# A linear-attention and mixture-of-experts kernel on one core: the order of its first part comes from a planner written into the kernel, and some of its transfers are merged or cut

## The chip, the core and the metric

The kernel runs on one core of one Trainium2 chip. The core has a matrix engine (TensorE, PE in the profile), a vector engine (VectorE, DVE), a scalar engine (ScalarE, ACT), a general engine (GpSimd, POOL) and an engine that here only issues transfers (SyncE, SP). Each engine runs its own list of instructions strictly in the order in which it was built; an instruction whose input is not there yet holds up everything behind it on that engine. The metric is device time in microseconds (us); lower is better. The number to predict is the median of several runs.

## What is computed

The reference is linear attention, a gated two-matrix product, and a layer of eight experts of which each token uses one:

```python
proj = einsum('bhsd,df->bhsf', x, w_phi)                 # for x = q and x = k
proj = proj - max(abs(proj), axis=-1)
phi  = concat([exp(proj), exp(-proj)])                   # q_p and k_p
kv, z = einsum('bhsf,bhsd->bhfd', k_p, v), sum(k_p, axis=2)
x = (q_p @ kv) / (q_p @ z + 1e-6)                        # 8 batches, 8 heads, 576 tokens of 64
x = ((x @ w1) * (x @ w2) @ w3) @ w_out                   # 4608 tokens of 512, inner width 1024
gate = softmax(x @ w_gate)                               # 8 experts, the largest one is used
out[tokens of e] = gate * (relu(x @ e_w1[e]) @ e_w2[e])  # inner width 1024
```

## The kernel before

To keep float32 accuracy with 16-bit matmuls, every operand is held as two float16 halves (high and low), and each product is three matmuls. ScalarE writes a high half, VectorE computes the low half as value minus high half; so most steps are a pair ScalarE, then VectorE.

The program has two parts. **The first part** runs four units of two batches. Each unit has four attention groups of two heads (`group`): q, k and v are loaded, split into halves on VectorE (`split`, lines 491 and 493, tile `sp`), turned by a transposing transfer (line 499, tiles `Tkf` and `Tqf`), projected on TensorE, exponentiated on ScalarE (`e`, `k`, `q`, lines 554 and 556; their low halves on VectorE, line 561), and multiplied (`kv`, `nm`, `nx`). The float32 tiles of k and of q share one buffer (`tag="kqf", bufs=1`), so the load of one waits for the splits of the other. Three blocks of the gated product (`moe1`) follow each unit, a unit later: `pab` on TensorE (lines 806 to 808), `asb`, `gf`, `gt` on ScalarE and VectorE, then `py` (line 843), its copy `yb` out of the accumulator by ScalarE (line 850), and rows of 2052 bytes that are stored to memory (`rows_d`, lines 940 and 943). Beside both, `expert_weight` prepares the sixteen expert matrices: a 2 MB load into the one buffer `wf` (line 296), squares for a scale (line 302), then eight pieces `pc`, high half on ScalarE (line 321), low half on VectorE (line 325), stored to a scratch tensor `wscr` (line 327). Four buffers of one piece each hold `pc`. **The second part** (`phase_b`, lines 1127 to 1183) runs forty slots of 128 tokens through the experts with weights loaded back from `wscr` (`wb`, 4 MB each); the first two of these loads are issued before the first part has ended. Its order is written out by hand.

In the first part each step is recorded with a time of its own, `at(t, fn)`, from the table `O`; the steps are traced in the order of these times. The framework then schedules: whenever an engine is free in its cost model, the ready instruction that was traced earliest is taken. What comes out is a fixed list for each engine. All transfers but the gathers and scatters go out from SyncE, in one list too.

## Time and profile before

| what | value |
|---|---|
| runs of the kernel | 1642.35, 1636.98, 1639.8 us; median 1639.8 |
| profiled execution, its own time | 1653.94 us |
| its span, first to last instruction | 1652.2 us |
| mean granted clock of TensorE | 0.936 of full speed |
| TensorE, VectorE, ScalarE busy over the span | 86%, 61%, 53% |
| transfers issued by SyncE in the change's reach | 16 loads `wf`, 128 stores `wscr`, 128 large loads of q and k |

The profile was taken in one execution, whose own time is 14 us above the median; differences worked out from it are taken off the median. The busy shares are means over two very different parts: in the first VectorE and TensorE are both loaded, in the second TensorE alone. They say little until they are read stretch by stretch.

### The profile page before, as it was taken

How to read it: one execution, taken by the hardware profiler on the slowest of the kernel's cores; microseconds unless marked ns; L12 is line 12 of the kernel's file. 1: busy time of each engine (PE TensorE's matmuls, PEld its weight loads, DVE VectorE, ACT ScalarE, POOL GpSimd, SP SyncE). 2: the span in 40 equal slices, each digit the busy share in tenths (PEclk: the TensorE clock that was granted, in tenths of full speed). 3: DMA queues.
4: the chain of work that ended last, by engine and by line, in shares of the span. 5: the costliest groups of instructions: out<-in, count | busy, mean ns of one | idle time of the engine just before them, and what ended most of it. 6: DMA issues, size and time to landing. Idle time of an engine off the chain costs nothing. (4 is left out here: it accounts for less than half of the span.)

```text
span 1652.2 us, 38216 instructions
## 1 busy us (share of the span) xinstructions
PE 1428.4 (86%) x14850; PEld 1032.2 (62%) x14854; DVE 1001.4 (61%) x3031; ACT 881.7 (53%) x1979; POOL 226.9 (14%) x491
## 2 busy tenths in 40 slices
PE   5988877888898796889697998968949999999998
PEld 4665555666665474657475766636746777777775
DVE  6998899987898696879697898434411111111111
ACT  4786688777786685768576777335201111111111
POOL 3313100010111010100101000100102111121110
PEclk9988777998999798999898999979979999999999
DMA  7845245575767775574955665963346346747351
GB/s 200 237 125 157 73 124 100 153 124 126 134 170 124 123 166 66 159 146 115 149 159 97 161 101 139 188 191 116 51 145 193 76 83 172 250 104 178 78 170 31
DMA packets 273043, 225.16 MB, mean 136 GB/s; under 512 B 187221, under 2 KB 244825, under 8 KB 271706
## 3 DMA queue, kind: packets, MB, share of 16 engines
q1 hardware_dynamic: 265306, 202.71, 53.5%
q0 software_dynamic: 7552, 19.97, 4.2%
q8 instruction: 118, 1.93, 0.6%
q14 instruction: 67, 0.55, 0.2%
HBM read 261.22 MB, written 53.67 MB: 191 GB/s over the span
## 5 line engine op out<-in xcount | busy, mean ns | idle before, releaser
L806 PE MATMUL pab<-xT,w 128*128 128x384 f16 x768 | 258.8, 337 | 26.1 <-ACT asb L813 16.1
L1132 DVE SCALAR_TENSOR_TENSOR hT<-ph,hT 128x512 f16<-128x512 f32 x80 | 55.3, 692 | 362.6 <-ACT hT L1131 362.6
L807 PE MATMUL pab<-xT,w 128*128 128x384 f16 x768 | 258.8, 337 | 0.0
L808 PE MATMUL pab<-xT,w 128*128 128x384 f16 x768 | 258.3, 336 | 0.0
L1127 PE MATMUL ph<-xTb,wb 128*128 128x128 f16 x1280 | 218.4, 220 | 22.6 <-DMA xTb<-rw 22.6
L843 PE MATMUL py<-w,gt 128*128 128x260 f16 (+1 forms) x1728 | 213.6, 278 | 16.5 <-ACT yb L850 12.1
L1128 PE MATMUL ph<-xTb,wb 128*128 128x128 f16 x1280 | 218.3, 220 | 0.0
L1129 PE MATMUL ph<-xTb,wb 128*128 128x128 f16 x1280 | 218.3, 220 | 0.0
L843 PEld LDWEIGHTS <-gt 128*128 128x128 f16 x1728 | 166.6, 100 | 43.3 <-issue 13.3
L1131 ACT ACTIVATE hT<-ph 128x512 f16<-128x512 f32 x80 | 47.8, 597 | 187.5 <-PE ph L1129 187.5
L1127 PEld LDWEIGHTS <-wb 128*128 128x128 f16 x1280 | 125.9, 98 | 27.9 <-DMA xTb<-rw 21.1
L1128 PEld LDWEIGHTS <-wb 128*128 128x128 f16 x1280 | 125.9, 98 | 4.5
L1129 PEld LDWEIGHTS <-wb 128*128 128x128 f16 x1280 | 125.9, 98 | 0.0
L1150 ACT ACTIVATE ob<-pob,scb 128x512 f32<-128x512 f32 x40 | 27.5, 687 | 183.4 <-PE pob L1148 183.4
L554 ACT ACTIVATE q<-pjT,nM 128x384 f16<-128x384 f32 x192 | 114.9, 598 | 17.2 <-PE nm L702 14.1
L702 PE MATMUL nm<-kvs,q 128*128 128x65 f16 (+1 forms) x1920 | 86.7, 201 | 41.3 <-DVE nx L712 37.4
L1146 PE MATMUL pob<-wb,hT 128*128 128x512 f16 x320 | 121.3, 379 | 0.0
L1147 PE MATMUL pob<-wb,hT 128*128 128x512 f16 x320 | 121.3, 379 | 0.0
L1148 PE MATMUL pob<-wb,hT 128*128 128x512 f16 x320 | 121.3, 379 | 0.0
L321 ACT ACTIVATE pc<-wf,ess 128x512 f16<-128x512 f32 x128 | 88.8, 726 | 57.2 <-DMA wscr<-pc 50.1
L556 ACT ACTIVATE e<-pjT,nM 128x384 f32<-128x384 f32 x192 | 116.0, 604 | 5.8 <-DVE q L561 5.8
L702 PEld LDWEIGHTS <-q 128*128 128x128 f16 (+1 forms) x1920 | 76.9, 104 | 66.1 <-issue 38.0
(255 smaller groups left out, 3237.5 us busy)
## 6 DMA issues: line engine op xcount, KB each, us to landing
wb<-wscr SPq DMA_DIRECT2D x40, 4096.0 KB
wf<-in_moe_w_dram SPq DMA_DIRECT2D x16, 2048.0 KB
wscr<-pc SPq DMA_DIRECT2D x128, 256.0 KB
raw<-in_moe_w_dram SPq DMA_DIRECT2D x32, 512.0 KB
rows_d<-row SPq DMA_DIRECT2D x32, 256.5 KB
kf<-in_k_dram SPq DMA_DIRECT2D x64, 128.0 KB
vf<-in_v_dram SPq DMA_DIRECT2D x64, 128.0 KB
qf<-in_q_dram SPq DMA_DIRECT2D x64, 128.0 KB
```

The costliest lines, as they stand in the source:

```text
L556: A.activation(e1, src, AF.Exp, scale=sgn * ES, bias=bias)
L702: T.matmul(nm[p0:p1, t, z, :], lhsT=hl[:, a, t, p0:p1], rhs=st["kvs"][:, b, h, z, bb, :], start=(a == b), stop=bool(a), skip_group_check=True)
L806: T.matmul(ps, lhsT=wh, rhs=xT[:, 0, kk], start=(kk == 0), stop=False)
L807: T.matmul(ps, lhsT=wh, rhs=xT[:, 1, kk], start=False, stop=False)
L808: T.matmul(ps, lhsT=wl, rhs=xT[:, 0, kk], start=False, stop=(kk == 3))
L843: T.matmul(py, lhsT=gT[i][:, a, t * P:(t + 1) * P], rhs=w34[:, i, b, hf, 0:cw], start=(i == 0 and a == b), stop=bool(i == 7 and a))
L1127: T.matmul(ph[:, mm, :], lhsT=wh, rhs=xT[:, 0, kk, :], start=(kk == 0), stop=False)
L1128: T.matmul(ph[:, mm, :], lhsT=wh, rhs=xT[:, 1, kk, :], start=False, stop=False)
L1129: T.matmul(ph[:, mm, :], lhsT=wl, rhs=xT[:, 0, kk, :], start=False, stop=(kk == 3))
L1146: T.matmul(po, lhsT=hT[:, 0, i2, :], rhs=wh, start=(i2 == 0), stop=False)
L1147: T.matmul(po, lhsT=hT[:, 0, i2, :], rhs=wl, start=False, stop=False)
L1148: T.matmul(po, lhsT=hT[:, 1, i2, :], rhs=wh, start=False, stop=(i2 == 7))
```

## The change

The change has two sides.

**Order.** `plan` takes all instructions of the first part as traced, works out which must wait for which (data, buffers, the pools that follow each other), gives each a duration and a distance to its followers (`Step`), and plays the program through: an engine takes the earliest traced instruction that is ready. Transfers of SyncE go through one queue, with at most eight in flight. The order that results is fixed with an edge from each instruction to the one before it on its engine. The table `O` is unchanged.

**Transfers.** The 2 MB load of an expert matrix becomes four of 512 KB, traced 0.4 steps of time apart; two pieces `pc` share a buffer and go out in one store of 512 KB (two buffers of two pieces, for four of one), in a layout in which they lie behind each other in `wscr`; the loads of two heads of q or k become one. In all SyncE issues 64 + 64 transfers fewer and 48 more.

```diff
+BYTES = {F32: 4, I32: 4, F16: 2, BF16: 2, U8: 1}
+OVERLAP = dict(DVE=80, Activation=105, Pool=-25)
+WAKE = 60
+LANES = 8
+SPARE = 0
+DMA_SPARE = 0
...
+        if self.dma:
+            b = n * 128 * BYTES.get(outs[0].dtype, 4)
+            if self.engine == "Pool":
+                self.hold, self.time = 1250, 10000
+            elif kind == "DmaTransposeAnt":
+                self.hold, self.queue, self.time = 1300, 1250, 2000
+            else:
+                self.hold, self.queue, self.time = 480, 100 + b / 280, 2000
+        elif kind == "Matmult":
+            n *= 4 if inns[0].dtype == F32 else 1
+            self.hold = max(28, n / 2.4 + 2) * 1.0
+            self.time = self.hold + 170
...
+        else:
+            if self.engine == "DVE":
+                t = 145 + n * (1.1 if two or psum or kind == "TensorReduce" else 0.6)
+            elif self.engine == "Pool":
+                t = 150 + n * (2.2 if two else 1.2)
...
+    lanes, queue = [0.0] * LANES, 0.0
...
+    for _ in steps:
+        t, e = min((max(free[e], 0.0 if takes[e] else waits[e][0][0]), e) for e in engines if takes[e] or waits[e])
+        while waits[e] and waits[e][0][0] <= t:
+            heapq.heappush(takes[e], heapq.heappop(waits[e])[1])
+        n = heapq.heappop(takes[e])
+        s = steps[n]
+        if s.dma and e == "SP":
+            t = max(t, lanes[0])
+            queue = max(queue, t + s.hold) + s.queue
+            end = queue + s.time
+            lanes = lanes[1:] + [end]
...
+        if e in prev:
+            tc.add_manual_dep(s.ins, prev[e].ins.name, info, reason="planned order")
+        prev[e] = s
...
-        [NE, P, 2, 2, 4096], F16, name="wscr")
+        [NE, P, 2, 8, 2, 512], F16, name="wscr")
...
-            nc.sync.dma_start(st["wf"].rearrange("p (k f) -> p k f", k=nk),
-                              src.rearrange("(k p) f -> p k f", p=P))
             st["cm"] = stat.tile([P, 4], F32, tag="ecm", name="ecm")
+
+        def load_part(j):
+            k0, kn = j * nk // 4, nk // 4
+            nc.sync.dma_start(st["wf"].rearrange("p (k f) -> p k f", k=nk)[:, k0:k0 + kn, :],
+                              src[k0 * P:(k0 + kn) * P, :].rearrange("(k p) f -> p k f", p=P))
...
         def piece_hi(j):
-            st["pc", j] = pools["prep"].tile([P, 2, 512], F16, tag="pc", bufs=4, name="pc")
+            if j % 2 == 0:
+                st["pp", j // 2] = pools["prep"].tile([P, 2, 2, 512], F16, tag="pc", bufs=2, name="pc")
+            st["pc", j] = st["pp", j // 2][:, j % 2]
             A.activation(st["pc", j][:, 0, :], st["wf"][:, j * 512:(j + 1) * 512], AF.Copy, scale=st["s"][:, 0:1])
 
         def piece_lo(j):
             pc = st["pc", j]
             V.scalar_tensor_tensor(pc[:, 1, :], st["wf"][:, j * 512:(j + 1) * 512], st["s"][:, 0:1], pc[:, 0, :],
                                    op0=ALU.mult, op1=ALU.subtract)
-            nc.sync.dma_start(wscr[e, :, idx, :, j * 512:(j + 1) * 512], pc)
+            if j % 2:
+                nc.sync.dma_start(wscr[e, :, idx, j - 1:j + 1], st["pp", j // 2])
 
         at(t0, load)
         for j in range(4):
+            at(t0 + 0.4 * j, load_part, j)
             at(t0 + O["e_sq"] + O["e_sq_j"] * j, square, j)
...
             for bb, b in enumerate(bs):
-                for h in range(2):
-                    nc.sync.dma_start(
-                        t[:, h, 5 * bb:5 * bb + 4, :],
-                        src[b, h0 + h, 0:512, :].rearrange("(p r) d -> p r d", r=4))
+                nc.sync.dma_start(
+                    t[:, :, 5 * bb:5 * bb + 4, :].rearrange("p h r d -> p h (r d)"),
+                    src[b, h0:h0 + 2, 0:512, :].rearrange("h (p r) d -> p h (r d)", r=4))
                 nc.sync.dma_start(
                     t[64 * bb:64 * bb + 64, :, 4, :],
                     src[b, h0:h0 + 2, 512:S, :].rearrange("h p d -> p h d"))
...
+    def plan_a():
+        body = max(nc.cur_f.blocks, key=lambda b: len(b.instructions))
+        plan(tc, list(body.instructions), (("su", "mp"), ("att", "wb"), ("att", "tb")))
+    at(t_end + 0.99, plan_a)
```

The lines below are of the built programs, 183 to 190 lines further down in the source of the changed kernel (line 491 of before is 681 there).

VectorE in the middle of the third unit, around one split of q (`sp<-qf`, line 491), before:

```order
L561 TENSOR_TENSOR q_10264<-e_10266,q_10264 128x384
L824 TENSOR_TENSOR gt<-gf,gt 128x384
L561 TENSOR_TENSOR q_10334<-e_10336,q_10334 128x384
L491 TENSOR_SCALAR sp<-qf 128x6x64
L561 TENSOR_TENSOR q_10338<-e_10340,q_10338 128x384
L638 SCALAR_TENSOR_TENSOR kvs<-kv,kvs 128x130 x2
```

The same split in the changed kernel, with the last of what stands ahead of it:

```order
L911 TENSOR_TENSOR rec<-rec,svi 128x6
L762 TENSOR_TENSOR pm<-pj,mk 128x384
L913 TENSOR_TENSOR xn<-nx,rec 128x2x3x64
L751 TENSOR_TENSOR q_10391<-e_10393,q_10391 128x384
L901 TENSOR_TENSOR nx<-nm,wq 128x195
L751 TENSOR_TENSOR q_10460<-e_10462,q_10460 128x384
L902 TENSOR_TENSOR nx<-nx,nm 128x195
L1007 TENSOR_TENSOR gf<-pab,asb 128x384
L751 TENSOR_TENSOR q_10464<-e_10466,q_10464 128x384
L372 TENSOR_SCALAR vsc<-pv 128x1
L681 TENSOR_SCALAR sp<-qf 128x6x64
L492 TENSOR_REDUCE ecs<-ecm 128x1
```

Twenty-eight instructions that stood behind the split stand ahead of it now, and none has gone the other way. Sixteen of them are of 384 elements (eight of line 561; two each of `gf`, `mk` and `pm`; one `gt`, one `xn`), six are `nx` of 195 elements, six are small.

ScalarE after the attention has ended, in the last unit's first block of the gated product, around the first piece of the last matrix but two, before:

```order
L850 COPY yb<-py 128x260 x2
L855 ACTIVATE junk,ssy<-yb 128x512
L321 ACTIVATE pc<-wf,ess 128x512
L850 COPY yb<-py 128x260
L321 ACTIVATE pc<-wf,ess 128x512 x3
L850 COPY yb<-py 128x260 x3
L898 ACTIVATE du<-du 128x24
L813 ACTIVATE asb<-pab 128x384
```

The same place in the changed kernel:

```order
L1040 COPY yb<-py 128x260 x2
L1045 ACTIVATE junk,ssy<-yb 128x512
L1040 COPY yb<-py 128x260 x4
L1088 ACTIVATE du<-du 128x24
L1003 ACTIVATE asb<-pab 128x384
L1011 CAST gt<-gf 128x384
L509 ACTIVATE pc<-wf,ess 128x512 x2
L1003 ACTIVATE asb<-pab 128x384
L509 ACTIVATE pc<-wf,ess 128x512 x2
```

The piece that stood ahead of the last four copies `yb` stands behind them now, and behind the first steps of the next block.

SyncE around one load of an expert matrix (`wf`), in the third unit just ahead of the split above, before:

```order
L327 DMA wscr<-pc 128x2x512
L296 DMA wf<-in_moe_w_dram 128x4x1024
L499 DMA_TRANSPOSE Tkf<-sp 128x6x128
L508 DMA vf<-in_v_dram 128x256
L510 DMA vf<-in_v_dram 64x64
L943 DMA rows_d<-row 128x1026 x3
L499 DMA_TRANSPOSE Tkf<-sp 128x6x128
L481 DMA qf<-in_q_dram 128x256 x2
L484 DMA qf<-in_q_dram 64x2x64
```

And in the changed kernel:

```order
L516 DMA wscr<-pc 128x2048
L483 DMA wf<-in_moe_w_dram 128x1024 x4
L689 DMA_TRANSPOSE Tkf<-sp 128x6x128
L1133 DMA rows_d<-row 128x1026 x3
L689 DMA_TRANSPOSE Tkf<-sp 128x6x128
L671 DMA qf<-in_q_dram 128x2x256
L674 DMA qf<-in_q_dram 64x2x64
```

The four parts of the load stand directly behind each other, where the one load stood; the row stores and the loads of q still follow it, the latter in half as many large transfers.

## Rows read from the trace of the kernel before

**Rows 1.** Page: span; busy us, share, instructions by engine

```profile
span 1652.2 us, 38216 instructions
...
PE 1428.4 (86%) x14850; PEld 1032.2 (62%) x14854; DVE 1001.4 (61%) x3031; ACT 881.7 (53%) x1979; POOL 226.9 (14%) x491
```

**Rows 2.** Stretches: length; busy (xn) PE, PEld, DVE, ACT, POOL; clock, DMA, GB/s

```profile
60.00:1050.00 990.00, 837.19 (x8854) 599.74 (x8857) 840.36 (x2618) 723.68 (x1683) 117.84 (x338) 0.91 0.62 132
200.00:300.00 100.00, 78.43 (x840) 55.49 (x838) 92.50 (x292) 82.68 (x204) 5.18 (x30) 0.79 0.49 115
1050.00:1205.00 155.00, 128.57 (x975) 89.80 (x973) 62.34 (x205) 52.54 (x113) 12.00 (x15) 0.93 0.53 137
1205.00:1230.00 25.00, 9.14 (x105) 8.20 (x106) 1.61 (x4) 1.19 (x2) 1.95 (x2) 0.60 0.55 173
1230.00:1652.00 422.00, 414.78 (x4697) 301.98 (x4695) 56.57 (x117) 74.05 (x118) 76.88 (x78) 1.00 0.50 134
```

**Rows 3.** VectorE's waits, 60 to 1050 us: us in total, times, longest

```profile
DVE sp L491 <- DMA qf<-in_q_dram: 23.3, 4, 16.6
DVE k L561 <- ACT e L556: 18.5, 12, 10.0
DVE q L561 <- ACT e L556: 17.9, 25, 7.4
DVE sp L491 <- DMA Tkf<-sp: 17.6, 5, 7.4
...
DVE sp L491 <- DMA Tqf<-sp: 7.9, 2, 7.4
```

**Rows 4.** VectorE in order of time; in brackets the idle before

```profile
617.93 0.56 DVE L561 TENSOR_TENSOR q<-e,q 128x384 f16<-128x384 f32 x1 [0.33 <-ACT e L556]
635.09 0.36 DVE L491 TENSOR_SCALAR sp<-qf 128x384 f16<-128x384 f32 x1 [16.61 <-DMA qf<-in_q_dram]
```

**Rows 5.** VectorE's groups by line, 60 to 1050 us: busy us, mean ns

```profile
L561 DVE TENSOR_TENSOR q<-e,q 128x384 f16<-128x384 f32 x192 | 106.1, 556 | 18.4 <-ACT e L556 17.9
...
L711 DVE TENSOR_TENSOR nx<-nm,wq 128x195 f32<-128x195 f32 x96 | 34.0, 354 | 9.0 <-PE nm L702 6.0 <-PE pab L807 2.0 <-remote 0.8
```

**Rows 6.** DMA issues of SyncE in order of time, from 602 us

```profile
602.72 0.47 SPq L296 DMA_DIRECT2D wf<-in_moe_w_dram  x1
...
612.61 1.91 SPq L943 DMA_DIRECT2D rows_d<-row  x3
...
616.27 1.03 SPq L481 DMA_DIRECT2D qf<-in_q_dram  x2
...
626.66 0.63 SPq L484 DMA_DIRECT2D qf<-in_q_dram  x1
```

**Rows 7.** View of rows 2: three 512 KB loads; one 2 MB load; stores

```profile
4.00:6.00 2.00, 0.00 (x0) 0.00 (x0) 0.00 (x0) 0.76 (x2) 1.20 (x5) 1.00 1.02 365
604.00:610.00 6.00, 5.97 (x68) 4.28 (x66) 6.00 (x25) 2.66 (x7) 1.05 (x3) 1.00 0.99 341
612.00:627.00 15.00, 10.45 (x98) 6.69 (x98) 5.58 (x22) 11.16 (x27) 4.59 (x9) 1.00 1.05 76
```

**Rows 8.** ScalarE's waits for transfers, 60 to 1050 us

```profile
ACT pc L321 <- DMA wscr<-pc: 25.7, 11, 10.0
ACT junk L302 <- DMA wf<-in_moe_w_dram: 24.8, 8, 11.8
```

**Rows 9.** ScalarE's waits for transfers, 1050 to 1205 us

```profile
ACT pc L321 <- DMA wscr<-pc: 24.4, 2, 17.9
```

**Rows 10.** TensorE's longest wait between 1050 and 1205 us, in order of time

```profile
1084.46 4.80 PE L843 MATMUL py<-w,gt 128*128 128x260 f16 x24 [12.13 <-ACT yb L850]
```

More of the change, by code (lines that the diff above doesn't have):

```diff
@@ L1 @@
+import heapq
+from collections import defaultdict
 from contextlib import ExitStack
@@ L61, with sizes, __init__, cells @@
 E23 = float(2 ** 23)
+BYTES = {F32: 4, I32: 4, F16: 2, BF16: 2, U8: 1}
[4 more added lines that the diff above has]
+DMA_SPARE = 0
+def sizes(ap):
+    n, span = 1, 1
+    for step, count in ap.ap[1:]:
+        n *= count
+        span += (count - 1) * abs(step)
+    return n, span
+class Step:
+    def __init__(self, ins):
+        self.ins, self.engine = ins, str(ins.engine).rsplit(".", 1)[-1]
+        kind = type(ins).__name__.removeprefix("Inst")
+        self.dma = "DMA" in kind.upper()
+        outs = [a for a in ins.outs if hasattr(a, "bass_ap")]
+        inns = [a for a in ins.ins if hasattr(a, "bass_ap")]
+        self.reads, self.writes = [self.cells(a) for a in inns], [self.cells(a) for a in outs]
+        n = max(sizes(a)[0] for a in (outs if kind != "TensorReduce" else inns)) if outs else 1
+        psum = any(c[0] == "P" for c in self.reads)
+        two = sum(sizes(a)[0] > 1 for a in inns) > 1
+        self.queue = 0.0
+        if self.dma:
[10 more added lines that the diff above has]
+            self.time = self.hold + 170
+            self.spare = SPARE if sizes(outs[0])[0] < 20 else 0
+        else:
[3 more added lines that the diff above has]
+                t = 150 + n * (2.2 if two else 1.2)
+            else:
+                t = 200 + 0.93 * n
+            if len(outs) > 1:
+                t += 190
+            self.hold, self.time = max(62, t - OVERLAP[self.engine]), t
+        self.after, self.begins, self.left, self.ready, self.start = [], [], 0, 0.0, 0.0
+    @staticmethod
+    def cells(a):
+        ap = a.bass_ap
+        t = ap.tensor
+        where = str(getattr(t, "space", "DRAM")).rsplit(".", 1)[-1][0]
+        if not hasattr(t, "tag"):
+            return ("D", t.name, None, ())
+        if where != "S":
+            return (where, t.name, t, (0,))
+        b = BYTES.get(a.dtype, 4)
+        row = t.bytes() // 128
+        lo = ap.offset * b % row
+        p0 = ap.offset * b // row
+        hi = lo + sizes(a)[1] * b
+        halves = [h for h, on in ((0, p0 < 64), (1, p0 + ap.ap[0][1] > 64)) if on]
+        return ("S", t.name, t, tuple((k, h) for k in range(lo // 32, (hi - 1) // 32 + 1) for h in halves))
@@ L1164, in phase_b @@
         slot_in(1)
-        V.tensor_copy(wb[1][:, 0, 0, 0:1], xq[1][:, 0, 0, 0:1])
+        V.tensor_copy(wb[1][:, 0, 0, 0, 0:1], xq[1][:, 0, 0, 0:1])
         next_w(1, 0)
```

107 lines of the change are left out of this document (97 added, 10 removed).

## Prediction

> **What bounds the kernel now.** I read the page first, then the table by stretches, then the waits of the two engines that the stretches point to, then single places in order of time. On the page [rows 1] TensorE is busy 86% of 1652.2 us and VectorE 61%; that mixes two parts. The stretches [rows 2] separate them. From 1230 us on TensorE is busy 414.78 of 422 us at full clock: the second part is matmul alone, its order is untouched, and I leave it and the 25 us of handover at their lengths. From 60 to 1050 us VectorE is busy 840.36 and TensorE 837.19 of 990 us, 85% each, neither full. The reader is to see there two engines that keep stopping each other. In 200 to 300 us VectorE reaches 92.5%: so well can it be fed. From 1050 to 1205 us VectorE has little left (62.34 of 155) and TensorE, at 128.57, sets the end.
>
> VectorE's 149.6 us of idle time (990 − 840.36) have two kinds of long waits [rows 3]. First, the splits of q and k wait for transfers: 23.3 us for the load of q, 17.6 and 7.9 us for transposes whose buffers the split needs. One of them alone is 16.61 us [rows 4]: the split `sp<-qf` stands at the head of VectorE's list from 618.5 to 635.1 us, while behind it the subtraction of line 561 has its inputs. Second, low halves wait for ScalarE (18.5 and 17.9 us), with one wait of 10.0 and one of 7.4. ScalarE then stood itself: for a store of pieces (longest 10.0) and for a load of an expert matrix (longest 11.8) [rows 8].
>
> Why q was late is in SyncE's list [rows 6]. The 2 MB load went out at 602.72, three row stores at 612.61, the loads of q from 616.27, the last of them only at 626.66. The load of 2 MB keeps the transfer engines 99% busy at 341 GB/s; the 15 us from the row stores on are as busy, but move 76 GB/s [rows 7]. So the transfers are late by some 10 us whatever the order on VectorE is.
>
> **The change, part by part.**
>
> *Splits of q and k.* The order of the change puts 28 instructions ahead of the split that waited 16.61 us. Sixteen of them are of 384 elements, 0.556 us each by line 561, and six are `nx`, 0.354 us each [rows 5]: 16 × 0.556 + 6 × 0.354 = 11.0 us, about 12 with the small ones. They fill 12 of the 16.6. The other waits for q and its transposes, 23.3 + 7.9 − 16.6 = 14.6 us in five, are shorter than such a block; I count 14 of them. The splits of k move less, a few instructions each; I count a third of 17.6, 6 us. Sum 32, bounds 16 (half) and 48.8 (all).
>
> *Waits behind ScalarE.* The waits of 10.0 and 7.4 us arise where a piece and a square stood at the head of ScalarE's list [rows 3, 8]. The changed order puts seven and nine exponentials and copies ahead of them (not shown); at the length of line 561 [rows 5] that is 16 × 0.556 = 8.9, and I count 8 of the 17.4 us. Bounds 0 and 17.4.
>
> *What of these 40 us reaches the end.* TensorE is as busy as VectorE [rows 2], so a gap that closes on one can open on the other. With 40 us less, VectorE would be at 840.36 / 950 = 88.5%, still under the 92.5% seen. I take three quarters, **30 us**; bounds a third and all.
>
> *The tail.* After the attention, ScalarE waited 24.4 us in two goes for stores of pieces, once 17.9 us [rows 9]: the two 4 MB loads for the second part were in the queue ahead of the stores. Behind that piece stood the copy `yb`, and TensorE stood 12.13 us for it [rows 10]. In the changed order the four copies and the next `asb` stand ahead of the piece. TensorE sets the end here, so the gap comes off whole: **12 us**; bounds 0 (another wait in its place) and 12.1. What is late next is the piece itself, and with it the last two matrices; the second part needs them only for its third stream of weights.
>
> *Other waits.* 149.6 − 48.8 − 17.4 = 83 us of VectorE's idle time are short waits for ScalarE and TensorE. Nearly every neighbourhood is reordered, and neither sign can be read from the order. I take 0, with 20 us either way, a quarter of them.
>
> *Loads cut in four.* The first square can start after a quarter of the load; this is inside the 8 us above. But the parts stand behind each other in SyncE's list, so what is queued behind them waits as long as before. Is a cut load slower? Three loads of 512 KB issued one after another ran at 365 GB/s, a 2 MB load at 341 [rows 7]: no, cost 0. The Trainium skill ("DMA: Bandwidth & Descriptors", section "Measured (HBM→SBUF, 128 partitions, SWDGE, issued from GpSimd)") advises 1 MiB or more in a transfer, which speaks against this cut; by the 2.0 us fixed plus bytes over 436 GB/s of its section "Anatomy of one DMA — SWDGE (gpsimd) path" I estimate 6 us more for each matrix, 96 us of queue in all. These rows, for transfers that overlap, don't show such a fixed part.
>
> *Stores and loads merged.* 80 issues fewer on SyncE, about half a microsecond each [rows 6]; SyncE mostly waits itself, so 0. The same bytes go out. Pieces wait for stores 25.7 + 24.4 us in 13 goes [rows 8, 9]; between the ends of losing these waits to other work and of more of them (below) I leave them.
>
> *Sum.* −30 − 12 = −42 us. For the profiled execution 1653.94 − 42 = 1611.9 (span 1610). Its own time is 14.1 us above the median of the runs, 1639.8; off the median the forecast is **1598 us**, 1580 to 1615 with the bounds of the large terms.
>
> **Rivals.**
>
> *The waits move.* The late transfers stay late. The tiles of k and q share one buffer, so a split that is held back holds back the next load, and the wait returns at the next split of k. Then a third of the 40 us is left and little of the tail: −15, **1625 us**. For it: the row stores and the load stand ahead of q in the list as before. Against: one split is moved by 12 us, not by a group, which lasts some 60 (990 us for sixteen).
>
> *Well fed throughout.* VectorE reaches the 92.5% of 200 to 300 us over all of the 990: 840.36 / 0.925 = 908.5, −81.5, and the tail: **1546 us**. For it: the costs in `Step` are near the rows (145 + 1.1 × 384 = 567 ns for line 561, 556 measured). Against: the planner knows nothing of the 76 GB/s after row stores, and it counts matmuls at full clock, where 200 to 300 us had 0.79.
>
> *Cut loads hold the queue.* Each extra start leaves the transfer engines idle for an issue, 0.47 us [rows 6]; 48 × 0.47 = 23 us of queue, −42 + 23 = −19, **1621 us**. Against it are the 365 GB/s. By the fixed part on the Trainium skill's page "DMA: Bandwidth & Descriptors" it would be −42 + 96, 1694 us.
>
> *No change.* The gains and new waits cancel within 0.3%, 4.9 us, which is about what a measurement of this kernel can tell from no change: **1640 us**.
>
> *Slower: pairs of pieces.* With two buffers of two pieces, the first store of a matrix leaves one piece later, and the fifth piece waits for 512 KB to land, not 256. Twice for each of the sixteen matrices ScalarE would stand, with the exponentials behind it, and VectorE behind these. Today 13 goes cost 50.1 us, the longest 10.0 and 17.9 [rows 8, 9]. At 4 us each, 32 goes are 128 us, 78 more than today: −42 + 78 = +36, **1676 us**. It decides from (42 + 50.1) / 32 = 2.9 us each. Against: the pieces of a pair stand together in the changed order, with other work up to the next pair.
>
> **How the numbers follow.** Forecast 0.42, waits move 0.22, well fed 0.11, cut loads 0.04, no change 0.08, pairs 0.13. The likeliest is 1598. The range reaches down to 1550, just short of the well-fed case, and up to 1645, past no change; that leaves out the pairs and about half of the well-fed case, some 2 in 10. Faster by over 0.3%: 0.42 + 0.22 + 0.11 + 0.04 = 0.79; within 0.3%: 0.08; slower: 0.13.
>
> **What would show it.** Right: no wait of VectorE's splits for q above 5 us; the stretch of 990 us shortened by 20 to 40 at 88% busy VectorE; no wait of TensorE for `yb` above 2 us; the second part unchanged. For the rivals: waits of the k splits in place of those of q; ScalarE's waits for stores of pieces grown past 50 us; a 2 MB load that takes longer than 6 us from its first part to its last. Wrong it would be if the planner's distances fit the short waits much better than I allow, or if its transfers, two microseconds away in `Step`, land so late that new instructions stand at the heads of the lists.

## The result, and the profile after

The changed kernel takes 1623.59 us (median of 5 runs, 1620.46 to 1627.92) where the kernel before took 1641.07 beside it (5 runs, 1636.98 to 1642.35): a ratio of 0.9895, 95% interval 0.9868 to 0.9922. On another chip it was 1628.52 to 1647.92, ratio 0.9893 (0.9864 to 0.9922). So it is faster, by 17 to 19 us; I had forecast 42. The range held it, the size was wrong.

The head of the page of the changed kernel; it answers to [rows 1].

```profile
span 1621.9 us, 38088 instructions
PE 1422.3 (88%) x14851; PEld 1037.0 (64%) x14854; DVE 1003.3 (62%) x3031; ACT 883.8 (54%) x1979; POOL 220.0 (14%) x491
```

The span is 30.3 us shorter than that of [rows 1], the medians only 17.5: the profiled execution of before was a long one, that of the changed kernel is its median. Next the table by stretches, which answers to [rows 2] (columns as there; the rows start at the same times as there).

```profile
60.00:1050.00 990.00, 848.20 (x8938) 615.02 (x8940) 846.22 (x2621) 727.62 (x1688) 113.53 (x338) 0.91 0.66 140
200.00:300.00 100.00, 76.77 (x855) 54.82 (x854) 96.17 (x299) 85.95 (x211) 7.57 (x34) 0.80 0.50 121
1205.00:1230.00 25.00, 22.80 (x272) 16.92 (x270) 3.24 (x7) 4.36 (x7) 7.82 (x8) 1.00 0.60 140
1230.00:1621.00 391.00, 386.23 (x4373) 281.20 (x4370) 53.29 (x111) 69.04 (x110) 69.27 (x70) 1.00 0.50 132
```

The second part is as it was: TensorE is busy in 386.23 of 391 us, and from its first matmul `ph` to the end it takes 431.3 us in both profiles. It begins earlier; at 1205 us the matmuls of the second part run, where before there was a handover. In 200 to 300 us VectorE is fed still better, 96.17 of 100.

VectorE's waits from 60 to 1050 us in the changed kernel (total us, times, longest), which answer to [rows 3]. Lines moved: the split of line 491 is line 681 now, line 561 is 751, and so on.

```profile
DVE pc L513 <- ACT pc L509: 20.2, 7, 7.4
DVE nx L901 <- PE nm L892: 16.0, 21, 2.0
DVE sp L681 <- DMA Tkf<-sp: 13.4, 3, 6.3
DVE mk L756 <- PE pj L738: 12.5, 7, 4.9
DVE xs L966 <- DMA xT<-xs: 11.9, 2, 11.4
...
DVE sp L681 <- DMA Tqf<-sp: 9.1, 3, 3.2
DVE q L751 <- ACT e L746: 7.8, 17, 1.6
...
DVE k L751 <- ACT e L746: 3.8, 6, 2.0
```

The waits for the load of q are gone (23.3 us in four before), those for exponentials fell from 36.4 us to 11.6. In their place stand waits that were smaller before. These are the same three groups of the kernel before:

```profile
DVE pc L325 <- ACT pc L321: 8.2, 6, 4.4
...
DVE nx L711 <- PE nm L702: 6.0, 9, 2.0
...
DVE mk L566 <- PE pj L548: 4.9, 3, 3.6
```

They grew by 12.0, 10.0 and 7.6 us. ScalarE's waits for stores of pieces in the same stretch, which answer to [rows 8], stayed at 25 us, in fewer and longer goes:

```profile
ACT pc L509 <- DMA wscr<-pc: 25.2, 4, 8.2
```

**Where the time came from.** I cut the first part at the last `xn`, the end of the attention, and at the first matmul `ph` of the second part. The attention ended at 1025.8 us before and ends at 995.0 now. The stretch from there to `ph`, the tail, is 195 us in both. The stretches of the tail in the kernel before and in the changed kernel, and below them the same in a second profile of each (of the first and fourth experiment):

```profile
1025.80:1220.90 195.10, 152.81 (x1131) 104.55 (x1129) 81.16 (x270) 67.44 (x145) 18.33 (x23) 0.90 0.55 127
```

```profile
995.00:1190.60 195.60, 153.01 (x1122) 104.18 (x1123) 82.37 (x271) 67.91 (x144) 16.71 (x22) 0.89 0.53 128
```

```profile
1022.00:1212.90 190.90, 152.50 (x1134) 104.22 (x1133) 81.14 (x270) 67.45 (x145) 18.28 (x23) 0.90 0.55 129
```

```profile
998.50:1193.80 195.30, 152.92 (x1123) 104.12 (x1124) 82.39 (x272) 68.01 (x144) 16.68 (x22) 0.89 0.55 128
```

TensorE has the same work in all four, 152.5 to 153 us. The attention gained 30.8 and 23.5 us, the tail lost 0.5 and 4.4. The 12.13 us that TensorE stood for `yb` [rows 10] are gone; a new gap took their place. VectorE, TensorE and SyncE of the changed kernel, in order of time:

```profile
1008.71 0.56 DVE L1014 TENSOR_TENSOR gt<-gf,gt 128x384 f16<-128x384 f32 x1 [0.58 <-ACT gt L1011]
1020.63 0.48 DVE L966 TENSOR_SCALAR xs<-xn,xss 128x512 f16<-128x512 f32 x1 [11.36 <-DMA xT<-xs]
```

```profile
1023.61 0.48 PE L996 MATMUL pab<-xT,w 128*128 128x384 f16 x1 [8.34 <-DVE gf L1007]
```

```profile
997.53 2.62 SPq L972 DMA_TRANSPOSE xT<-xs  x2
1000.24 1.73 SPq L1133 DMA_DIRECT2D rows_d<-row  x3
1002.95 25.15 SPq L972 DMA_TRANSPOSE xT<-xs  x5
1028.26 0.94 SPq L1199 DMA_DIRECT2D wb<-wscr  x2
```

Three row stores are issued at 1000.24 us, the transposes of the next block behind them. VectorE stands 11.36 us for one of these transposes, and TensorE stands behind VectorE. It is the picture of [rows 6, 7] again at another place: row stores, then late transfers. While they are under way the transfer engines are full and move little (busy share 1.14, 92 GB/s):

```profile
1000.20:1013.00 12.80, 12.12 (x60) 6.61 (x61) 5.01 (x10) 4.58 (x9) 3.12 (x5) 0.77 1.14 92
```

### The profile page after: what moved, and what is told of

Its sections match the earlier page's. It is cut to its first block, busy times and chain, and to the rows that moved or that the text cites. A ratio compares the mean times of both kernels' runs of the same rounds, so it can differ in the third digit from the quotient of the medians.

```text
span 1621.9 us, 38088 instructions
## 1 busy us (share of the span) xinstructions
PE 1422.3 (88%) x14851; PEld 1037.0 (64%) x14854; DVE 1003.3 (62%) x3031; ACT 883.8 (54%) x1979; POOL 220.0 (14%) x491
## 5 line engine op out<-in xcount | busy, mean ns | idle before, releaser
L996 PE MATMUL pab<-xT,w 128*128 128x384 f16 x768 | 262.7, 342 | 22.8 <-DMA xT<-xs 8.3
L997 PE MATMUL pab<-xT,w 128*128 128x384 f16 x768 | 262.2, 341 | 0.0
L998 PE MATMUL pab<-xT,w 128*128 128x384 f16 x768 | 262.1, 341 | 0.0
L1033 PE MATMUL py<-w,gt 128*128 128x260 f16 (+1 forms) x1728 | 210.0, 275 | 2.4 <-ACT gt L1011 1.4
L1033 PEld LDWEIGHTS <-gt 128*128 128x128 f16 x1728 | 165.1, 99 | 24.8 <-ACT gt L1011 1.6
L816 PE MATMUL kv<-vs,k 128*128 128x65 f16 x1920 | 97.6, 201 | 32.7 <-ACT k L794 13.8
L816 PEld LDWEIGHTS <-k 128*128 128x128 f16 x1920 | 87.0, 103 | 59.4 <-DVE k L799 16.4
L997 PEld LDWEIGHTS <-w 128*128 128x128 f16 x768 | 78.5, 102 | 59.5 <-issue 24.1
## 6 DMA issues: line engine op xcount, KB each, us to landing
rows_d<-row SPq DMA_DIRECT2D x32, 256.5 KB
```

Source lines behind the costliest of these rows:

```text
L816: T.matmul(kv[:, bb, z, :], lhsT=hl[:, a, t, :], rhs=vs[:, tv, b, :], start=False, stop=bool(end and a), skip_group_check=True)
L996: T.matmul(ps, lhsT=wh, rhs=xT[:, 0, kk], start=(kk == 0), stop=False)
L997: T.matmul(ps, lhsT=wh, rhs=xT[:, 1, kk], start=False, stop=False)
L998: T.matmul(ps, lhsT=wl, rhs=xT[:, 0, kk], start=False, stop=(kk == 3))
L1033: T.matmul(py, lhsT=gT[i][:, a, t * P:(t + 1) * P], rhs=w34[:, i, b, hf, 0:cw], start=(i == 0 and a == b), stop=bool(i == 7 and a))
```

## The experiments

Theory P: the profile of before was an unusual execution, so what I took from it was too large. Theory W: the transfers that row stores make late stay late, and what was removed came back as other waits. Theory T, its case in the tail: the gain at `yb` was given back because of the row stores at 1000 us. Chips differ (the medians of before were 1648.37, 1647.92, 1644.99, 1634.94 and 1647.30 us in the five sets below), so kernels of different sets are compared by their ratio to before. All times are medians. Each planned kernel is planned anew, so an edit that concerns one transfer moves other instructions too; where it matters, the text says how many.

```
set  kernel                              us       ratio to before (95%)
1    before, second profile              1645.72  (before: 1648.37, 17 runs, 1636.96 to 1653.96)
1    order only                          1632.80  0.9907 (0.9872 to 0.9942)
1    transfers only                      1644.11  0.9984 (0.9959 to 1.0008)
1    row stores by GpSimd                1611.56  0.9782 (0.9741 to 0.9823)
2    the changed kernel again            1628.52  0.9893 (0.9864 to 0.9922)
2    three row stores of the tail late   1620.99  0.9838 (0.9809 to 0.9868)
2    all row stores late                 1589.51  0.9640 (0.9613 to 0.9667)
2    transfers planned 6 us away         1634.25  0.9905 (0.9874 to 0.9936)
3    row stores apart                    1604.74  0.9739 (0.9698 to 0.9780)
3    row stores late, together           1609.73  0.9795 (0.9754 to 0.9836)
3    row pitch 2112, changed kernel      1600.12  0.9721 (0.9674 to 0.9769)
3    row pitch 2112, kernel before       1629.88  0.9905 (0.9878 to 0.9933)
4    late, pitch 2112                    1570.44  0.9596 (0.9568 to 0.9624)
4    late, whole loads                   1589.50  0.9721 (0.9693 to 0.9749)
4    late, single pieces                 1584.68  0.9690 (0.9660 to 0.9719)
5    all row stores late, again          1589.01  0.9653 (0.9627 to 0.9679)
5    late, pitch 2112, again             1576.88  0.9572 (0.9544 to 0.9601)
5    late, pitch, transfers of before    1591.07  0.9663 (0.9636 to 0.9690)
```

**The kernel before, a second profile.** No edit.

> The kernel before, unchanged, profiled a second time. Theory P (the first profile of before, at 1653.94 us, 13 us above the median of its runs, held stalls that most executions do not have): this execution ends near 1641 us, the waits of VectorE's q splits for the load of q between 60 and 1050 us come to 12 us or less (23.3 in the first profile), and the wait of 16.61 us at 618 us is under 8 us. Theory W (the stalls are there in every execution; what was removed came back as other waits): the waits for the load of q are again 20 us or more, the one at 618 us is above 13 us, and the attention groups end within 3 us of where they ended in the first profile, also if the whole is shorter.

It took 1645.72 us. VectorE's waits:

```profile
DVE sp L491 <- DMA qf<-in_q_dram: 19.6, 4, 12.1
DVE k L561 <- ACT e L556: 18.8, 13, 6.0
DVE sp L491 <- DMA Tkf<-sp: 17.2, 5, 7.8
```

The waits for the load of q come to 19.6 us (23.3 in [rows 3]), those for `Tkf` to 17.2 (17.6). The long wait is 12.1 us where it was 16.61. The stalls are there each time, to within some microseconds; the ends of the attention differ by 3.8 us, the lengths of the tails by 4.2. Theory W's three marks (20, 13 and 3 us) are each missed by a little, theory P's (12 and 8 us) by more. Theory P falls as far as it concerns the stalls. What remains of it: over 17 runs on one chip this kernel spreads from 1636.96 to 1653.96 us with a median of 1648.37, so 1653.94 was at the upper end, but the 1639.8 of three runs was at the lower.

**Order alone, transfers alone.** The first takes the planner into the kernel before and leaves its transfers; the second leaves the planning out of the changed kernel:

```
-    at(t_end + 0.99, plan_a)
```

> The kernel before with the planned order alone: loads of expert matrices whole, pieces stored one by one, four loads for a tile of k or q. If the order carries the change (my step 'splits of q and k', and cut loads and merged stores at 0): 1620 to 1628 us, ratio 0.987 to 0.992. Rival, the transfers carry a good part of it (80 issues fewer on SyncE, squares that start on a quarter of the matrix): 1630 to 1640 us.

> The changed kernel with the planning left out, so with the order of before and the changed transfers. If the order carries the change: 1637 to 1645 us, ratio within 0.3% of 1. Rival, the transfers carry part of it: 1625 to 1636 us. If cut loads or pairs of pieces cost something that the order then hides: above 1646 us.

The order brings 0.93%, the transfers 0.16%, which is no more than the measurement can tell; together they bring 1.05 to 1.07%. The order carries the change. (The 1632.80 us of the order alone lie in the rival's range, its ratio of 0.9907 in the first theory's; on a chip whose kernel before takes 1648.37 us the ratio is what counts.) With the transfers alone VectorE's waits for the load of q are even longer in its profile:

```profile
DVE sp L681 <- DMA qf<-in_q_dram: 41.3, 6, 16.1
```

**The changed kernel again.**

> The changed kernel, unchanged, timed on the same chip as the three below and profiled again. If its executions spread as those of the kernel before do (1636.96 to 1653.96 us over 17): some 10 us between the fastest and the slowest, median 1620 to 1630, ratio 0.985 to 0.990. If the change also took the spread away: all within 5 us of 1623.

Its runs spread from 1625.69 to 1634.24 us, half as far as those of before beside it (1640.34 to 1656.26; 6 runs, though, to 11). Its tail is the fourth row of the tails above.

**Three row stores of the tail later.** Up to the end of the attention every list is as in the changed kernel; then SyncE's list has nine transposes ahead of these stores where it had four:

```
+    tail = [s for s in steps if any(w[1].startswith("rows_d") for w in s.writes)][-13:-10]
+    [setattr(s, "late", 16000) for s in tail]
...
-            heapq.heappush(waits[o.engine], (o.ready, m))
+            heapq.heappush(waits[o.engine], (o.ready + o.late, m))
```

> The changed kernel, in which the planner counts three row stores at the end of the attention as ready 16 us later; so five transposes of the first block after the attention stand ahead of these stores in SyncE's list, not behind them; up to there all lists are as they were. Theory T (the 12 us of the yb wait were gained, and given back because this block's transposes were late behind the row stores): the wait of VectorE for the transposed tile (11.36 us) and of TensorE behind it (8.34 us) fall under 2 us, from the end of the attention to the first matmul of the second part it takes 180 to 186 us in place of 195.6, and the median falls by 8 to 15 us. Rival (that stretch is set by something else, and a gap closed in it opens elsewhere, as it did before): still 191 to 198 us, and the median within 4 us of the changed kernel's.

It gained 7.5 us against the changed kernel on the same chip, just short of the 8 of theory T. TensorE's waits from 998 to 1045 us, and the tail:

```profile
PE pab L996 <- DMA xT<-xs: 4.4, 1, 4.4
PE pr L1087 <- DVE oh L1075: 2.8, 1, 2.8
PE pab L996 <- DVE gf L1007: 0.4, 1, 0.4
```

```profile
998.40:1187.40 189.00, 151.38 (x1123) 103.69 (x1124) 82.54 (x271) 67.64 (x144) 16.90 (x22) 0.90 0.55 132
```

TensorE's 8.34 us are 0.4 now. VectorE still waits 3.5 us for one of these transposes, where theory T said under 2. Of the 195.3 us of the tail 189.0 are left, between theory T's range and the rival's. So the row stores ahead of the transposes took back about half of the 12 us at `yb`. That the other half was lost to them too is not shown.

**All row stores later.** The planner counts a row store as ready 10 us later. Since it also lets a store begin only after the one ahead of it has begun, each is planned 10 us behind the last, and in the trace they go out mostly 5 to 20 us apart: late and apart.

```
+        self.late = 10000 if any(w[1].startswith("rows_d") for w in self.writes) else 0
...
-            heapq.heappush(waits[o.engine], (o.ready, m))
+            heapq.heappush(waits[o.engine], (o.ready + o.late, m))
```

> The changed kernel, in which the planner counts every row store as ready 10 us later, so that transposes and loads that come ready meanwhile go ahead of it. Theory W (row stores ahead of transposes make the waits for transposed tiles that are left): 12 to 25 us under the changed kernel, about the kernel with the row stores issued by GpSimd, 1605 to 1612. Rival (only the place at the end of the attention counts): as much as the run with three stores moved, no more. Rival (the stores meet other transposes later instead): within 4 us of the changed kernel.

It gained 39.0 us against the changed kernel, far more than I expected of it; with that it is 58 us under the kernel before. Only the time at which the planner counts the row stores as ready was changed. The plan that follows has other differences too: some 250 of VectorE's 2910 instructions ahead of the second part and 95 of ScalarE's 1858 stand elsewhere. So it is shown that moving the row stores in the plan brings 39 us, as theory W would have it; that all of it comes from the transfers behind them is not. From 560 to 950 us, the changed kernel and then this one:

```profile
560.00:950.00 390.00, 333.30 (x3655) 247.82 (x3653) 328.61 (x1062) 281.06 (x656) 38.59 (x135) 0.93 0.71 139
```

```profile
560.00:950.00 390.00, 348.71 (x3902) 259.86 (x3901) 345.34 (x1108) 299.73 (x701) 42.86 (x139) 0.95 0.62 142
```

Both engines are busier by 15 to 17 us in 390, while the transfer engines are busy for less of the time (0.62 for 0.71) and move as much. VectorE's waits for `Tkf` and `Tqf` are no longer among its longest; the first there are

```profile
DVE q L751 <- ACT e L746: 17.0, 25, 5.6
DVE gf L1007 <- PE pab L998: 15.4, 8, 3.6
DVE nx L901 <- PE nm L892: 13.2, 22, 2.3
```

**Row stores by another queue.** `nc.gpsimd.dma_start` for the two calls of `nc.sync.dma_start` in `row_out`.

> The changed kernel with the row stores (three for every group and pair, 24 KB to 260 KB into the rows in DRAM) issued by GpSimd in place of SyncE; order planned again with that. Theory W (transposes and loads that stand behind the row stores in SyncE's list are late by some 10 us, and that is what sets the waits that are left): 1603 to 1615 us, and no single wait of VectorE or TensorE for a transposed tile above 5 us between 60 and 1050 us. Rival W2 (the row stores and the transposes disturb each other in the transfer engines, whichever queue they are issued from): within 5 us of 1624, with the waits for transposed tiles still there. Theory P alone: within 5 us of 1624, with few such waits in either kernel.

The ratio is 0.9782 where the changed kernel's is 0.9893: some 18 us, inside theory W's range, but its other mark fails, for single waits for transposed tiles of 5 us and more remain. TensorE waits 10.1 us for one `Tkf`:

```profile
PE pj L737 <- DMA Tkf<-sp: 25.4, 5, 10.1
```

The stores of this run are 256.5 and 128.2 KB, three or four to a block, and still go out together. By the trace's packet records (more on them below) the three stores issued from 597 us on take 13.5 us from the first packet to the last, those from 840 us on 14.0, and one that is alone 0.8 to 1.7. Being out of SyncE's list helps; it is not all, and the mechanism of rival W2, that the stores disturb the transfer engines whichever queue they come from, is there as well.

**Transfers planned farther away.** `self.time` of SyncE's transfers 6000 in place of 2000.

> The changed kernel, in which the planner counts on 6 us from the transfer queue to landing where it had 2. If the planner's short transfers put instructions at the heads of the lists whose data are not there (what I named last as a way to be wrong): 10 to 20 us faster than the changed kernel, and the waits for transfers and transposed tiles between 60 and 1050 us at half or less. Rival (what makes a transfer late are single jams of 10 us and more, which no fixed distance describes): within 5 us of the changed kernel, either way.

It is 5.7 us slower than the changed kernel by the medians, and the intervals of the ratios overlap. The short fixed distance, which I had named as a way to be wrong, is not what cost the gain.

**Apart, or late?** Two things were changed at once by the late stores. One kernel puts the stores of a block apart without delaying the first (in its trace 2 to 24 us), the other delays them together and has SyncE take the stores of a block one right behind the other:

```
+    [setattr(steps[n], "late", 5000 * k) for n, k in zip(rows, (0, 1, 2, 0, 1, 1, 2, 0, 1, 2) * 4)]
...
```

```
+    [setattr(steps[n], "late", 10000) for i in (0, 3, 7) for n in rows[i::10]]
...
+        [deps[n].update(set().union(*(deps[m] for m in q))) for n in q]
...
```

> The changed kernel, in which the planner puts the row stores of a block apart: the first as early as before, each next one 5 us after the one ahead of it has started. Theory J1 (row stores that are under way together slow each other down, 298 ns for a packet of 2052 bytes in place of 86 when one store is alone, and all that is queued behind waits; the gain of the run with the late stores came from their being 10 us apart): 1588 to 1602 us. Theory J2 (transposes issued right behind a store slow it down and are slowed; the gain came from letting them pass): the first store still stands ahead of transposes, so at most half of the gain, 1608 to 1628.

> The changed kernel, in which the row stores of a block are planned 10 us later, but all of a block together, one right behind the other. Theory J1 (stores together slow each other): 1612 to 1630 us, and packets of stores still at 200 ns and more. Theory J2 (only the transposes behind them matter): 1585 to 1597, as with stores late one by one.

Neither theory is right alone: both times lie outside both theories' ranges. Against the changed kernel's ratio, apart brings 1.5% and late together 1.0%, of the 2.5% that both bring. That the stores slow each other also where no transpose is near is seen at the end of the changed kernel's first part. First one store alone, then four with three stores of pieces, in the view of transfers (a row of shares and one of GB/s in 40 slices of the stretch, then sums):

```profile
GB/s 0 0 0 0 0 0 0 0 0 0 0 0 0 0 192 383 383 410 410 301 383 356 410 219 55 0 0 0 0 0 0 0 0 0 0 0 0 0 0 0
DMA packets 144, 0.26 MB, mean 88 GB/s; under 512 B 16, under 2 KB 16, under 8 KB 144
...
rows_d<-row SPq DMA_DIRECT2D x1, 256.5 KB
```

```profile
GB/s 0 0 421 410 386 316 375 334 201 176 340 305 111 117 59 100 29 94 76 47 41 70 76 129 94 71 94 94 70 70 105 70 64 105 70 129 105 35 59 47
DMA packets 835, 1.92 MB, mean 137 GB/s; under 512 B 174, under 2 KB 174, under 8 KB 835
...
wscr<-pc SPq DMA_DIRECT2D x3, 512.0 KB
rows_d<-row SPq DMA_DIRECT2D x2, 256.5 KB
rows_d<-row SPq DMA_DIRECT2D x2, 128.2 KB
```

The one alone goes at some 383 GB/s and is done in less than a microsecond (3 us in 40 slices). In the other stretch (14 us) the pieces start at the same rate; then the rest goes at 29 to 129 GB/s for the 9 us that are left. No transpose is issued there. The trace also has a record for each packet; the mean length of those of 2052 bytes (2112 with the wide pitch) from 300 to 1000 us:

```
before 239 ns (second profile 198)    the changed kernel 298 (301)
all row stores late 102 (107)         late, together 194        apart 187
pitch 2112, changed kernel 298        pitch 2112, before 164    late, pitch 123 to 126
```

A packet of a store that is alone takes 86 ns.

**The pitch of the rows.** A row is 2052 bytes, and the three stores of a block write rows that are neighbours. With 30 halves more each begins at a multiple of 64 bytes:

```
-ROWW = 2 * DM + 2
+ROWW = 2 * DM + 32
...
+            G.memset(row[:, 2 * DM + 2:ROWW], 0.0)
```

> The changed kernel with rows of 2112 bytes in DRAM in place of 2052 (30 more halves in each row, set to zero by GpSimd, stored and read back with it), so that every row begins at a multiple of 64 bytes; the stores go together as in the changed kernel. Theory J1a (stores of a block write neighbouring rows at the same time, and rows that share a piece of memory of 64 bytes hold each other up): packets near 90 ns, 1588 to 1602 us. Rival J1b (stores together are slow for another reason): packets still at 200 ns and more, within 5 us of the changed kernel, 1623 to 1633.

> The kernel before with rows of 2112 bytes, its order and transfers as they were. If J1a holds and the jams were also what made the stalls of the kernel before: 1610 to 1630 us, the waits of VectorE for the load of q under 8 us (23.3 in its profile). If the jams cost only where the planner has closed the other gaps: 1640 to 1650. If J1b holds: no change, 1643 to 1652.

The time came out as theory J1a has it, by 1.7% under the changed kernel, and in the kernel before by 0.95%. The packets came out as J1b has it in the first (298 ns as before) and between the two in the second (164 for 198 to 239). J1a's other mark, VectorE's waits for the load of q under 8 us, fails in the kernel before:

```profile
DVE sp L491 <- DMA qf<-in_q_dram: 21.0, 4, 14.5
```

Group by group the picture is mixed. In the kernel before, four of the first nine groups of stores have packets of 90 to 96 ns with the pitch, near those of a store alone, where the same groups had 122 to 326 ns without it; in the changed kernel it is two of nine (94 and 103 ns for 131 and 135). So the wider pitch helps, but not, or not only, in the way I thought. That it is the pitch and not a new order can be seen in the changed kernel: with the pitch SyncE's list ahead of the second part is the same and only some 4 of VectorE's 2910 instructions stand elsewhere, yet the attention ends at 978.4 us, where without it it ends at 995.0 and 998.5. What in the pitch does it stays open. With the same pitch in both, the change is worth 29.8 us on one chip (1629.88 to 1600.12), where without it it is worth 17 to 19.

**Late and wide together**, first on one chip with the next two, then again beside the late stores alone.

> The row stores late and 10 us apart, as in the run with late stores (1589.5 us), and with rows of 2112 bytes as in the run with that pitch (1600.1). If both only take away the same loss (row stores that are slow while they go out together): 1584 to 1593 us, no more than the late stores alone. If the pitch does something of its own (in reading the rows back, or in single stores): 1565 to 1580.

> The kernel with late row stores, unchanged, timed again beside the one with the wider pitch, since the kernel before itself differed by 10 us between the chips of the last runs (1634.9 to 1648.4). If pitch and lateness take away one loss: within 5 us of the one with the pitch. If the pitch adds: 10 to 20 us slower than it.

> The kernel with late row stores and the wider pitch, unchanged, timed again, with a new profile: ratio to before 0.957 to 0.962 as in its first run. The difference to the run with late stores alone is as above.

On one chip the pitch takes 12.1 us off the late stores (1589.01 to 1576.88): it removes a loss of its own (some 40 of VectorE's 2910 instructions stand elsewhere here). One part of it shows at the handover, where the first matmul of the second part waits for rows that are read back; TensorE without and with the pitch:

```profile
PE ph L1318 <- DMA xTb<-rw: 20.2, 1, 20.2
```

```profile
PE ph L1318 <- DMA xTb<-rw: 16.5, 1, 16.5
```

That is 3.7 of the 12.1 us. In the same two profiles the attention ends 5.7 us earlier with the pitch, and the tail is 7.1 us shorter, these 3.7 included. This kernel is the fastest of the study, 4.0 to 4.3% under the kernel before and, by the ratios, 3.0 to 3.3% under the changed one.

**The transfers, with the stores out of the way.** Whole loads: `load_part` moves all `nk` rows and is called once. Single pieces: four buffers of one piece and a store for each, as before. Transfers of before: these two, four loads for a tile of k or q, and the layout of `wscr` as before.

> The run with late stores (1589.5 us), with the expert matrices loaded by one transfer of 2 MB each in place of four of 512 KB. My step 'cut loads, cost 0, gain inside the 8 us of the waits behind ScalarE': 1589 to 1598 us. Rival (cut loads hold the queue, 0.47 us for each extra issue, 23 us in all): 1566 to 1580.

> The run with late stores (1589.5 us), with each piece stored by itself from four buffers, as before, in place of pairs from two. My step 'merged stores 0': 1585 to 1594 us. Rival (pairs hold ScalarE up, the case that I gave for slower): 1565 to 1582. If the fewer issues on SyncE are worth something: 1595 to 1605.

> Late row stores and the wider pitch with the planned order, but with the transfers of the kernel before: whole loads of expert matrices, pieces stored one by one, four loads for a tile of k or q. My steps put cut loads and merged stores at 0: within 5 us of the run with both. Rival (with the jams gone the transfers matter, as they did not before): 8 us slower or more. Rival (cut loads and pairs cost, and the order hides it): 8 us faster or more.

On one chip the transfers of before cost 14.2 us (1591.07 to 1576.88). The other two ran in the fourth set, on a chip that ran the same kernel with late stores and pitch in 1570.44 where the fifth took 1576.88; times 1576.88 / 1570.44 they are 1596.0 and 1591.2, beside 1589.01 for what they are edits of: 7 us for the whole loads, 2 for the single pieces. By their ratios to before (0.9721 and 0.9690 for 0.9653) it is 11 and 6 us; the intervals of the first two are apart, those of the single pieces and of the late stores overlap. So whole loads cost 7 to 11 us, and single pieces 2 to 6, not to be told from nothing. The loads of k and q were not undone by themselves, so how the rest divides stays open.

## Why the prediction was wrong in its size

**Splits and waits behind ScalarE, 30 us: right in one pair of profiles, 6.5 us too much in the other.** The end of the attention moved by 30.8 us in one pair of profiles and by 23.5 in the other; the second pair, whose spans differ by 18.6 us, is the one like the medians, which differ by 17.5 and 19.4. No wait for the load of q is left, and the 959.2 us that in the first pair now correspond to the 990 have VectorE busy in 86.7% of the time, where I had said 88:

```profile
60.00:1019.20 959.20, 821.81 (x8767) 597.88 (x8769) 831.92 (x2591) 718.36 (x1670) 113.53 (x338) 0.91 0.66 135
```

But I was right in part by luck: the waits named gave 23.3 + 24.8 us, more than the 40 that I had counted on, and some 30 of VectorE's other waits came instead (20.2 + 16.0 + 12.5 us for 8.2 + 6.0 + 4.9). The term "other waits", which I had put at 0 with 20 us either way, was thus too small, and taking three quarters of the 40 happened to cover it.

**The tail, "so the gap comes off whole: 12 us": this step failed.** The gap at `yb` went, and the tail kept its length or grew (by 0.5 and 4.4 us); its lower bound, "another wait in its place", was what happened. I read only the wait that was removed and asked what `yb` is ahead of. I did not follow SyncE's list through the new order: three row stores now stood ahead of five transposes of the next block, where in the kernel before eight of nine transposes were out ahead of these stores. Moving these three stores alone gave 7.5 us back; why the rest of the 12 us did not come is not shown. The span was forecast as 1610 and was 1621.9; in this pair of profiles this term is the difference. In the second pair the attention misses 6.5 and the tail 16.4 of the 23.4 us that lie between the 42 forecast and the 18.6 that came. All four signs that I had named for being right were seen: they look at the gaps that were to go, and none at what would come in their place.

**The 14.1 us taken off "as the median of the runs": mis-sized.** I subtracted what lay between the profiled execution and the median of three runs. With more runs the median of before is 1645 to 1648 on most chips, so 6 to 9 us was nearer; and the profiled execution of the changed kernel was its median, so that there nothing was to be taken off. Together with the 11.7 us by which that execution missed its forecast, 11.7 + 14.1 = 25.8 us, it makes the 25.6 us between 1598 and 1623.6. The inner range, 1580 to 1615, does not follow from the bounds that I named either: a third to all of the 40 us and 0 to 12.1 for the tail make 1588 to 1626, which holds the result.

**"So the transfers are late by some 10 us whatever the order on VectorE is": the sentence was true, and I drew the wrong conclusion.** I took the lateness as given and asked only what could be put into the wait. The lateness is itself a matter of order: with the row stores late and apart the packets take 102 ns in place of 298, and the kernel takes 39 us less. The planner knows nothing of it (a transfer costs it 100 ns and its bytes), and moved the stores to places where their packets take longer than before (298 ns for 239 and 198). The rival "the waits move" had this in it and gave 1625. That its number fits is luck: it counted on a third of the 40 us, 13, and little of the tail, where 23.5 to 30.8 came and the tail gave nothing. Its own mechanism, waits of the splits of k in place of those of q, is seen only in part: the splits waited 13.4 us for `Tkf` (17.6 before), and TensorE waited longer for it, in the kernel before and then in the changed one:

```profile
PE pj L547 <- DMA Tkf<-sp: 10.9, 2, 6.2
```

```profile
PE pj L737 <- DMA Tkf<-sp: 20.3, 4, 5.9
```

**Cut loads 0, merged stores 0: right in this change, wrong beyond it.** Here the transfers are worth 0.16%. The 365 GB/s that I read for cut loads come from two microseconds at the start, in which loads of k went out as well; the loads of the change itself bear it out. By the packet records, the eight matrices that are read in rows of 4 KB take 6.7 us whole in the kernel before and 6.75 cut in the changed one (medians, first packet to last). With the stores out of the way the transfers are worth 14.2 us, half or more of which goes with the cut loads, by the estimate above. The Trainium skill ("DMA: Bandwidth & Descriptors", section "Measured (HBM→SBUF, 128 partitions, SWDGE, issued from GpSimd)") would have transfers of 1 MiB and more. By the fixed part on that page I had estimated 96 us against the cut. No run shows that: four loads of 512 KB are, if anything, 7 to 11 us faster here than one of 2 MB. Why is not shown. That the squares start on the first part is not it: ScalarE waits 26.2 us for these loads with the late stores and cut loads, 17.7 with whole ones (60 to 1200 us); with whole loads it is VectorE that waits longer for pieces (19.0 us for 6.1).

**Rivals that did not come.** ScalarE's waits for stores of pieces stayed at 25.2 us up to 1050 us, and the 24.4 us behind them in the tail [rows 9] are gone. VectorE's longer waits for pieces (20.2 us for 8.2) are not made by the pairs: with the planned order and single pieces they are as long (18.7 us). So pairs cost nothing that these runs show. The well-fed case (1546) was not reached by the change; late stores and the pitch, which are not part of it, reach 1570 to 1577.

## What to carry to other kernels

When a wait is to be removed by moving its victim, look at what makes the transfer late as well: here putting the row stores of a block apart, without delaying the first, was worth 1.5%, more than the whole new order (0.9%), and late and apart 2.5%; and with wider rows in both kernels the change was worth 29.8 us in place of 17 to 19. Name among the signs of being right also one that looks at what comes in the place of a gap. Follow the queue of the transfers through the new order as you follow the engines', for every gap you count on to come off whole. Take the distance of a profile from the median only from as many runs as the spread asks for, and profile each kernel twice.

## What the runs showed of the chip that I had not expected

Stores of 128 rows of 2052 bytes into neighbouring rows take 86 ns a packet when one is under way, and 131 to 472 ns on average when three or four are (the nine groups of the changed kernel up to 1012 us), with the other transfers behind them; a group lasts 4.5 to 15 us from the issue of its first store to its last packet, where its 788 KB at the 383 GB/s of a store alone would be 2.1 us. Issued by GpSimd, three together are as slow (13.5 and 14.0 us). Why they slow each other is open. The Trainium skill ("DMA: Bandwidth & Descriptors", section "How a descriptor splits into AXI transactions") says that a transfer which does not start at a multiple of 256 bytes has its first piece start at the boundary below, at extra cost; it says so of reading, and for these stores it would make one alone as slow as one among three, which the trace contradicts. A pitch of 2112 bytes, not a multiple of 256 either, took off 12 to 28 us in three kernels; in the one of 12.1 us, 3.7 showed where the rows are read back. Where the rest comes from is not shown. And one kernel differs between chips: before had medians of 1634.94 to 1648.37 us, and on each chip its runs spread over 12 to 20 us.
